# Delta-rule attention and a squared-Relu MLP on one core: the state's products with the queries moved behind T's second level, the key normalization moved to 0.45 to 0.80 of a period, and the weights' high words scaled in place

## The chip, the cores and the metric

The kernel runs on 1 core of one Trainium2 chip. The metric is the time of one execution on the device in microseconds (us). Before the change three runs took 672.78, 672.32 and 670.96 us (median 672.32).

## What is computed

Inputs are q, k and v of shape (4 batches, 8 heads, 768 tokens, 48), beta of shape (4, 8, 768), and two weight matrices. All arithmetic is to be that of float32; the weights are drawn in float64, so each of their elements is two 32-bit words.

```python
k_n = k / (np.linalg.norm(k, axis=-1, keepdims=True) + 1e-06)
for t in range(S):
    y[:, :, t] = einsum('bhd,bhde->bhe', q[:, :, t], state)
    v_old = einsum('bhde,bhd->bhe', state, k_n[:, :, t])
    state = state + beta_t * einsum('bhd,bhe->bhde', k_n[:, :, t], v[:, :, t] - v_old)
x = y.transpose(0, 2, 1, 3).reshape(B * S, H * D)      # 3072 x 384
h = maximum(x @ w_in, 0)                                # w_in 384 x 2048
out = (h * h) @ w_out                                   # w_out 2048 x 384
```

## The kernel before

**Chunks.** The 768 tokens are worked off in 12 units of 64 tokens. Within a unit the recurrence is written as matrix products: the keys' products with each other and with the queries (`static`, which also transposes keys and queries through TensorE and sends the blocks of the key products through DRAM), an inverse of a triangular matrix T per head, found by VectorE in 31 steps of two instructions on blocks of 32 (`invert`, lines 422 and 423), a second level that joins the blocks (`whole`), the products with the state carried over from the unit before (`on_state`), the solved values (`solved`), and the update of the state and the output (`onward`). The MLP (`moe`) then works on the 256 rows of the unit, with every operand split in a high and a low part, three products for one.

**Periods.** For unit `u` from 1 to 11 one period of the program weaves together: the MLP of unit u-1, the attention of unit u with the state, `static` and `invert` of unit u+1, and the loads and the key normalization of unit u+2. Each of these is a generator that gives up control after a piece of work, and each has a list of places between 0 and 1; `weave` sorts all pieces by place and writes them out in that order. The order on TensorE, VectorE, ScalarE and SyncE's DMA queue is this written order (`manual_schedule` names the four); GpSimd's is a scheduler's. The places are in 32nds for most parts: the MLP's pieces stand at 4/32 to 31/32 (its last ones in the next period, at 0/32 to 3/32 and 0.2), `static` at -1 and 4.9/32, the four pieces of the state part (`whole` in two, `solved`, `onward`) at 11.9/32, 15.9/32, 19.9/32 and 23.9/32, the inverse from 0.40 of one period to 0.12 of the next. In the period of unit 1 the rest of the weights is split too.

**Loads and normalization.** `loads(u)` first issues the keys of unit u+2 and the values of unit u+1, then the queries and beta, at two places between 0.22 and 0.42. Six places follow, N1, for the normalization: two of a square on ScalarE (line 270) with its sum on VectorE (271), the root on ScalarE (273), then VectorE's reciprocals and corrections (275 to 281) and the product that normalizes the keys (283). All loads of a period, the inverse's way through DRAM (`inv<-z`, `tt<-inv`, `t1t<-inv`), the blocks (`blocks<-ap`, `lt<-blocks`) and the output go through SyncE's queue, in the written order.

**The state part before the change.** At 11.9/32: 64 products for T's second level (line 461), ScalarE's copy of them, 64 products of the state with the queries into the bank `g`, 64 with the keys, and VectorE's subtraction of the latter from the values (501). At 15.9/32: the second 64 products of the level (471) and ScalarE's scaled copy of them into T's tile (475). At 19.9/32: T times the values (512) and its copy (514). At 23.9/32: the state's update (528, 531) and the output, added up in `g` (537, 541).

**The weights.** Each of 28 parts of the weights is loaded as pairs of words. `split_weights` makes a float32 high part and a low part of each: the absolute value of the high word on ScalarE (137), a maximum with 2^-15 on GpSimd (138), a shift and a mask on VectorE (145), the sign put back (148), the exponent alone (151), the low word scaled by it (152); then ScalarE and TensorE make the two parts (158, 165 to 167) and in the later parts VectorE takes a difference (172). The first 17 parts or so are split before the periods begin, the others in the period of unit 1.

Of the kernel before, what the change touches and what calls it, by code (L numbers as in the profile page):

```python
# [8 lines left out]
F32 = mybir.dt.float32  # L9
# [3 lines left out]
AF = mybir.ActivationFunctionType  # L13
ALU = mybir.AluOpType
AX = mybir.AxisListType

LEAST = 2.0 ** -15


@with_exitstack  # L20
def kernel(
# [22 lines left out]
    nc = tc.nc  # L44
    B, H, S, D = q.shape
    DM, DF = w_in.shape
    P = 128
    C = 64
    HB = 32
    NC = 2  # L50
    NP = H // 2
# [47 lines left out]
    state = const.tile([P, 2, NC, NP, D], F32, name="state")  # L99
# [11 lines left out]
    raws = []  # L111
# [14 lines left out]
    def room(x, n):  # L126
        pool, first, second = rooms[x % 2 if x < AHEAD - 1 else 0]
        return pool.tile([P, PC], I32, name=first)[:, :n], pool.tile([P, PC], I32, name=second)[:, :n]

    def split_weights():  # L130


        def least(x):

            w1 = raws[x][:, :, 1]
            a, rest = room(x, w1.shape[1])
            nc.scalar.activation(out=a.bitcast(F32), in_=w1.bitcast(F32), func=AF.Abs)  # L137
            nc.gpsimd.tensor_scalar(out=a.bitcast(F32), in0=a.bitcast(F32), scalar1=LEAST, scalar2=None, op0=ALU.max)  # L138
            return x, a, rest

        def words(x, a, rest):
            raw = raws[x]
            w1 = raw[:, :, 1]

            nc.vector.tensor_scalar(out=a, in0=a, scalar1=3, scalar2=0x3FFFFFF8,
                                    op0=ALU.logical_shift_left, op1=ALU.bitwise_and)

            nc.vector.scalar_tensor_tensor(out=a, in0=w1, scalar=-0x40000000, in1=a,  # L148
                                           op0=ALU.bitwise_and, op1=ALU.bitwise_or)

            nc.vector.tensor_scalar(out=w1, in0=a, scalar1=-0x800000, scalar2=None, op0=ALU.bitwise_and)
            nc.vector.scalar_tensor_tensor(out=rest.bitcast(F32R), in0=raw[:, :, 0].bitcast(U32), scalar=2.0 ** -52,
                                           in1=w1.bitcast(F32), op0=ALU.mult, op1=ALU.mult)
            return x, a, rest

        def high(x, a, rest):
            hl = wpool.tile([P, 2, raws[x].shape[1]], F32R, name=place[x])
            nc.scalar.copy(out=hl[:, 0], in_=a.bitcast(F32))
            return x, a, rest, hl

        def low(x, a, rest, hl, formed=False):
            ps = split_bank()[:, :hl.shape[2]]
            first = [(plus, hl[:, 1])] if formed else [(ident, a.bitcast(F32)), (minus, hl[:, 0])]
            for m, y in first:
                nc.tensor.matmul(ps, lhsT=m, rhs=y, start=(m is first[0][0]), stop=False)  # L165
            nc.tensor.matmul(ps, lhsT=plus, rhs=rest.bitcast(F32R), start=False, stop=True)
            nc.scalar.copy(out=hl[:, 1], in_=ps)
            halves[weight_parts[x][:2]] = hl[:, 0], hl[:, 1]

        def remainder(x, a, rest, hl):  # L170

            nc.vector.tensor_tensor(out=hl[:, 1], in0=a.bitcast(F32), in1=hl[:, 0].bitcast(F32), op=ALU.subtract)

        before, ready, x = None, [], 0
        while split_early:

            far = 3 if x < AHEAD - 3 else 1
            while len(ready) < far:
                ready.append(least(x + len(ready)))
            if x == 0:  # L180
                yield
            now = high(*words(*ready.pop(0)))
            if before:
                low(*before)
            before = now
            x += 1
            while len(ready) < (far if x < AHEAD - 3 else 1):
                ready.append(least(x + len(ready)))
            yield

        low(*before)
        before = None
        for x in range(x, NW):
            if before:
                remainder(*before)
            now = words(*ready.pop(0))
            yield
            if not ready and x + 1 < NW:
                ready.append(least(x + 1))
            yield  # L200
            if before:
                low(*before, formed=True)
            before = high(*now)
            yield
        remainder(*before)
        yield
        low(*before, formed=True)
        yield

    def split_bank():  # L210

        turn[1] += 1
        return (ps_o.tile([P, PC], F32, name=f"o{turn[1] % 2}") if split_early else ps_x.tile([P, PC], F32, name="x"))
# [72 lines left out]
    def x_tile(u=2):  # L286

        turn[0] += 1
        pool, name = (ps_h, "h") if u <= 1 and turn[0] % 4 >= 2 else (ps_x, "x")
        return pool.tile([P, PC], F32, name=name)  # L290
# [155 lines left out]
    def whole(d):  # L446

        u, ap = d["u"], d["ap"]
        tt = ttile[u % 2]
        upper = [slice(b * C, b * C + HB) for b in range(2)]  # L450
        lower = [slice(b * C + HB, (b + 1) * C) for b in range(2)]

        t1 = apool.tile([P, H, HB], F32, name="t1", bufs=1)
        nc.vector.transpose(out=t1, in_=d["t1t"])
        m = apool.tile([P, H, HB], F32, name="m", bufs=1)
        at = [upper, lower]
        ps = ps_h.tile([P, PC], F32, name="h")[:, :H * HB].rearrange("p (k t) -> p k t", k=H)
        for h in range(H2):
            c, e = h // H, h % H
            for b in range(2):  # L460
                nc.tensor.matmul(ps[at[h % 2][b], h // 2], lhsT=ap[lower[b], c, e, 0, :HB], rhs=tt[lower[b], c, e, HB:],
                                 start=True, stop=True)
        nc.scalar.copy(out=m, in_=ps)
        if u:
            on_state(d)
        yield
        ps = [x_tile(u)[:, :H * HB].rearrange("p (k t) -> p k t", k=H) for _ in range(2)]
        for h in range(H2):
            for b in range(2):
                rows = at[h % 2][b]  # L470
                nc.tensor.matmul(ps[h % 2][upper[b], h // 2], lhsT=t1[rows, h // 2], rhs=m[rows, h // 2], start=True, stop=True)  # L471
        right = tt.rearrange("p c (k j) t -> p j (c k) t", j=2)
        for j in range(2):
            for b in range(2):
                nc.scalar.mul(out=right[upper[b], j, :, HB:], in_=ps[j][upper[b]], mul=-1.0)  # L475
        yield

    def areas(two, n):

        return [x[:, :NC * n * D].rearrange("p (c n e) -> p c n e", c=NC, n=n) for x in two]  # L480

    def by_parity(x):

        return [x.rearrange("p c (n j) e -> p j c n e", j=2)[:, j] for j in range(2)]

    def on_state(d):

        kq, vt = d["kq"], d["vt"]
        d["g"] = g = ps_g.tile([P, 2, PC], F32, name="g")
        ks = areas([x_tile() for _ in range(2)], NP)  # L490
        for x, dst in ((1, areas([g[:, j] for j in range(2)], NP)), (0, ks)):
            for c in range(NC):
                for p in range(NP):
                    for j in range(2):
                        rows = slice(j * C, j * C + D)
                        for b in range(2):
                            to = slice((b ^ j) * C, ((b ^ j) + 1) * C)
                            nc.tensor.matmul(dst[j][to, c, p], lhsT=kq[rows, c, p, b, x], rhs=state[rows, b, c, p],  # L498
                                             start=(c == 0 and p == 0) if x else True, stop=not x, skip_group_check=True)
        for left, old in zip(by_parity(vt), ks):  # L500
            nc.vector.tensor_tensor(out=left, in0=left, in1=old, op=ALU.subtract)  # L501

    def solved(d):

# [146 lines left out]
    def state_part(d):  # L651
        yield from whole(d)
        solved(d)
        yield
        onward(d)
        yield
# [4 lines left out]
    STEPS = 32  # L661
    OVER = 4
    CHAIN = (11.9, 15.9, 19.9, 23.9)
    L1, N1 = (0.22, 0.42), (0.62, 0.92)
    I0, I1, NI = 0.40, 1.12, HB
    units = S // C
    ds_ = []
# [106 lines left out]
```

## Time and profile before

| | |
|---|---|
| runs | 672.78, 672.32, 670.96 us |
| profiled execution | 668.09 us, of which span 666.0 us |
| TensorE busy (matmuls) | 593.1 us, 89% of the span |
| VectorE busy | 434.7 us, 65% |
| ScalarE busy | 319.3 us, 48% |
| GpSimd busy | 73.7 us, 11% |
| TensorE's granted clock | 0.955 of full speed on average |
| moved by DMA | 49.92 MB in 173726 packets |

The profile names an instruction by the line of the kernel, its engine (PE is TensorE, PEld its loading of weights, DVE VectorE, ACT ScalarE, POOL GpSimd, SP SyncE, SPq the issue of a DMA on SyncE's queue), its operation, and the tiles it writes and reads. In a row of the timeline the first two numbers are the start and the time in us, and the brackets say how long the engine stood idle before it and what ended that. In a row of the groups stand the total busy time, the mean in ns, and the idle time before. In a row of the waits stand the total, the count and the longest. In a row of the stretches stand the stretch, its length, the busy time and count of PE, PEld, DVE, ACT and POOL, then the granted clock of TensorE, the DMA share and GB/s.

### The profile page before, as it was taken

The page shows a single profiled execution, that of the slowest core. Times are in us where ns is not written, and L with a number is a line of the kernel's source. Part 1 is how long each engine was busy: PE and PEld are TensorE (multiplying, and loading weights), DVE is VectorE, ACT ScalarE, POOL GpSimd, SP SyncE. Part 2 cuts the span into 40 slices and gives each one's busy share as a digit, 9 for nine tenths or more (in the row PEclk, how much of TensorE's full clock was granted, in tenths as well). Part 3 has the DMA queues.
Part 4 walks back from the last instruction along what each step waited for, and adds up shares of the span by engine and source line. Part 5 has one row for each costly group of instructions (what it writes and reads, how often), then busy time and mean ns, then how long its engine had stood idle before and what let it go on. Part 6 is the DMA issues. An engine that isn't in the chain of part 4 may idle for free.

```text
span 666.0 us, 23091 instructions
## 1 busy us (share of the span) xinstructions
PE 593.1 (89%) x9898; PEld 551.7 (83%) x9898; DVE 434.7 (65%) x1154; ACT 319.3 (48%) x620; POOL 73.7 (11%) x89
## 2 busy tenths in 40 slices
PE   0750788887999999999899999999999999999997
PEld 0530367887999899999899999999999998999996
DVE  4889887898568388397386595683883874841221
ACT  3740476564353453544355453544535554435442
POOL 6632333220100100101001001001001010000000
PEclk9965788788999999999899999999999999999999
DMA  7698622400450441532432523514514315030100
GB/s 157 158 234 298 198 52 46 77 2 1 72 112 10 95 89 19 103 69 34 100 55 39 102 49 56 112 22 78 104 23 104 68 28 111 2 65 2 25 1 25
DMA packets 173726, 49.92 MB, mean 75 GB/s; under 512 B 165424, under 2 KB 168504, under 8 KB 173624
## 3 DMA queue, kind: packets, MB, share of 16 engines
q1 hardware_dynamic: 171160, 47.85, 33.7%
q8 instruction: 78, 1.28, 0.8%
q10 hardware_dynamic: 2336, 0.59, 0.5%
q14 instruction: 24, 0.20, 0.1%
q0 software_dynamic: 128, 0.01, 0.0%
HBM read 37.32 MB, written 11.01 MB: 73 GB/s over the span
## 4 chain that ended last, share of the span: by engine, by line
PE 61%; DVE 19%; DMA 9%; SPq 4%; issue 4%; ACT 2%; DVEq 0%; ACTq 0%
PE h L588 24%; PE o L575 23%; DVE tmp L422 4%; DVE z L423 3%; DMA kpad<-in_k_dram 2%; DVE tt L423 2%; DVE h_h L420 2%; DVE h_l L567 2%; PE x L498 2%; PE g L498 1%; DMA blocks<-ap 1%; DMA inv<-z 1%; PE g L333 1%; DMA lt<-blocks 1%; PE x L333 1%
## 5 line engine op out<-in xcount | busy, mean ns | idle before, releaser
L575 PE MATMUL o<-w,h_h 128*128 128x384 f32 x768 | 200.0, 342 | 0.0
L588 PE MATMUL h<-x_h,w 128*128 128x256 f32 x1152 | 177.4, 290 | 0.0
L588 PEld LDWEIGHTS h<-x_h,w 128*128 128x128 f32 x1152 | 155.1, 193 | 3.6 <-issue 0.2
L595 ACT ACTIVATE r<-h 128x512 f32<-128x512 f32 x96 | 57.4, 598 | 194.5 <-PE h L588 193.9
L575 PEld LDWEIGHTS o<-w,h_h 128*128 128x128 f32 x768 | 136.3, 189 | 0.8
L567 DVE TENSOR_TENSOR h_l<-r,h_h 128x512 fp32r<-128x512 f32 x96 | 67.1, 699 | 99.1 <-PE o L575 61.2
L575 PE MATMUL o<-w,h_l 128*128 128x384 f32 x384 | 130.4, 340 | 0.0
L422 DVE SCALAR_TENSOR_TENSOR tmp<-lt,bt,z 128x126 f32<-128x126 f32 (+22 forms) x310 | 95.5, 308 | 50.7 <-DMA lt<-blocks 44.0
L588 PE MATMUL h<-x_l,w 128*128 128x256 f32 x576 | 100.9, 284 | 0.6 <-issue 0.6
L423 DVE TENSOR_TENSOR z<-z,tmp 128x126 f32<-128x126 f32 (+22 forms) x310 | 79.2, 255 | 10.7
L588 PEld LDWEIGHTS h<-x_l,w 128*128 128x128 f32 x576 | 83.2, 192 | 0.8 <-issue 0.8
L575 PEld LDWEIGHTS o<-w,h_l 128*128 128x128 f32 x384 | 72.5, 189 | 0.0
L596 ACT ACTIVATE r<-r 128x512 f32<-128x512 f32 x96 | 60.7, 633 | 3.0
L598 ACT CAST h_h<-r 128x512 fp32r<-128x512 f32 x96 | 59.6, 621 | 3.1
L406 POOL MEMSET z<- 128x512 f32 x10 | 5.3, 532 | 383.2 <-DMA inv<-z 383.2
L138 POOL TENSOR_SCALAR a<-a 128x384 f32<-128x384 f32 (+1 forms) x19 | 26.2, 1380 | 50.4 <-ACT a L137 46.5
L165 PE MATMUL o<-r,plus 128*128 128x512 f32 (+1 forms) x16 | 10.5, 745 | 18.6 <-DVE r L148 18.6
L501 DVE TENSOR_TENSOR vt<-vt,x 128x384 f32<-128x384 f32 x22 | 11.2, 549 | 15.2 <-PE x L498 15.2
L475 ACT ACTIVATE tt<-x 32x256 f32<-32x256 f32 x44 | 16.5, 374 | 9.6 <-PE x L471 9.0
L317 PE MATMUL x<-plus,kpad 64*128 64x64 f32 x104 | 7.8, 248 | 14.5 <-DMA kpad<-in_k_dram 12.4
L498 PE MATMUL x<-state,kq 48*64 48x48 f32 x704 | 14.1, 221 | 7.2 <-issue 7.2
L165 PEld LDWEIGHTS o<-r,plus 128*128 128x128 f32 x16 | 3.0, 234 | 20.2 <-ACT s L273 18.2
(134 smaller groups left out, 731.0 us busy)
## 6 DMA issues: line engine op xcount, KB each, us to landing
w<-in_moe_w_in_dram SPq DMA_DIRECT2D x12, 512.0 KB
w<-in_moe_w_out_dram SPq DMA_DIRECT2D x16, 384.0 KB
lt<-blocks SPq DMA_DIRECT2D x22, 256.0 KB
vt<-in_v_dram SPq DMA_DIRECT2D x48, 96.0 KB
out_dram<-a SPq DMA_DIRECT2D x46, 96.0 KB
kpad<-in_k_dram SPq DMA_DIRECT2D x88, 48.0 KB
qpad<-in_q_dram SPq DMA_DIRECT2D x88, 48.0 KB
blocks<-ap SPq DMA_DIRECT2D x48, 64.0 KB
```

The source lines that it names most:

```text
L138: nc.gpsimd.tensor_scalar(out=a.bitcast(F32), in0=a.bitcast(F32), scalar1=LEAST, scalar2=None, op0=ALU.max)
L165: nc.tensor.matmul(ps, lhsT=m, rhs=y, start=(m is first[0][0]), stop=False)
L422: nc.vector.scalar_tensor_tensor(out=tmp, scalar=bt[:, s:s + 1], op0=ALU.mult, op1=ALU.mult, **factors)
L423: nc.vector.tensor_tensor(out=z[:, :nj, s + 1:], in0=z[:, :nj, s + 1:], in1=tmp, op=ALU.subtract)
L475: nc.scalar.mul(out=right[upper[b], j, :, HB:], in_=ps[j][upper[b]], mul=-1.0)
L498: nc.tensor.matmul(dst[j][to, c, p], lhsT=kq[rows, c, p, b, x], rhs=state[rows, b, c, p], start=(c == 0 and p == 0) if x else True, stop=n ...
L567: nc.vector.tensor_tensor(out=h_l, in0=r, in1=h_h.bitcast(F32), op=ALU.subtract)
L575: nc.tensor.matmul(o[i], lhsT=a[:, e, i * P:(i + 1) * P], rhs=halves["wo", ft][w], start=(ft == 0 and n == 0), stop=(ft == FT - 1 and n == 2))
L588: nc.tensor.matmul(hp[:, e], lhsT=halves["wi", (kt, ft // EACH)][w][:, f], rhs=x[:, kt], start=(n == 0), stop=(n == 3 * KT - 1))
L595: nc.scalar.activation(out=r, in_=hp, func=AF.Relu)
L596: nc.scalar.activation(out=r, in_=r, func=AF.Square)
L598: nc.scalar.copy(out=h_h, in_=r)
```

## The change

Three things are changed. The products of the state with the queries go from the first piece of the state part to the second, behind the matmuls of line 471; `on_state` becomes a helper for either kind. The six places of the normalization go from 0.62 to 0.92 to 0.45 to 0.80 of the period. And the high word of each weight is no longer made absolute and bounded in a tile of its own: ScalarE multiplies it by 2^-112 in place, and VectorE shifts it from there; the sign is taken from the scaled word.

```diff
-LEAST = 2.0 ** -15
+DOWN = 2.0 ** -112
...
         def least(x):
-            w1 = raws[x][:, :, 1]
-            a, rest = room(x, w1.shape[1])
-            nc.scalar.activation(out=a.bitcast(F32), in_=w1.bitcast(F32), func=AF.Abs)
-            nc.gpsimd.tensor_scalar(out=a.bitcast(F32), in0=a.bitcast(F32), scalar1=LEAST, scalar2=None, op0=ALU.max)
-            return x, a, rest
-
-        def words(x, a, rest):
+            w1 = raws[x][:, :, 1].bitcast(F32)
+            nc.scalar.activation(out=w1, in_=w1, func=AF.Copy, scale=DOWN)
+            return x,
+
+        def words(x):
             raw = raws[x]
             w1 = raw[:, :, 1]
-            nc.vector.tensor_scalar(out=a, in0=a, scalar1=3, scalar2=0x3FFFFFF8,
-                                    op0=ALU.logical_shift_left, op1=ALU.bitwise_and)
-            nc.vector.scalar_tensor_tensor(out=a, in0=w1, scalar=-0x40000000, in1=a,
+            a, rest = room(x, w1.shape[1])
+            nc.vector.tensor_scalar(out=a, in0=w1, scalar1=3, scalar2=None, op0=ALU.logical_shift_left)
+            nc.vector.scalar_tensor_tensor(out=a, in0=w1, scalar=-0x80000000, in1=a,
                                            op0=ALU.bitwise_and, op1=ALU.bitwise_or)
...
         nc.scalar.copy(out=m, in_=ps)
         if u:
-            on_state(d)
+            keys_on_state(d)
         yield
...
                 nc.tensor.matmul(ps[h % 2][upper[b], h // 2], lhsT=t1[rows, h // 2], rhs=m[rows, h // 2], start=True, stop=True)
+        if u:
+            queries_on_state(d)
         right = tt.rearrange("p c (k j) t -> p j (c k) t", j=2)
...
-    def on_state(d):
-        kq, vt = d["kq"], d["vt"]
+    def on_state(d, x, dst):
+        for c in range(NC):
+            for p in range(NP):
+                for j in range(2):
+                    rows = slice(j * C, j * C + D)
+                    for b in range(2):
+                        to = slice((b ^ j) * C, ((b ^ j) + 1) * C)
+                        nc.tensor.matmul(dst[j][to, c, p], lhsT=d["kq"][rows, c, p, b, x], rhs=state[rows, b, c, p],
+                                         start=(c == 0 and p == 0) if x else True, stop=not x, skip_group_check=True)
+
+    def keys_on_state(d):
+        ks = areas([x_tile() for _ in range(2)], NP)
+        on_state(d, 0, ks)
+        for left, old in zip(by_parity(d["vt"]), ks):
+            nc.vector.tensor_tensor(out=left, in0=left, in1=old, op=ALU.subtract)
+
+    def queries_on_state(d):
         d["g"] = g = ps_g.tile([P, 2, PC], F32, name="g")
...
+        on_state(d, 1, areas([g[:, j] for j in range(2)], NP))
...
-    L1, N1 = (0.22, 0.42), (0.62, 0.92)
+    L1, N1 = (0.22, 0.42), (0.45, 0.80)
```

More of the change, by code (lines that the diff above doesn't have):

```diff
@@ L484, in by_parity @@
         return [x.rearrange("p c (n j) e -> p j c n e", j=2)[:, j] for j in range(2)]
-    def on_state(d):
-        kq, vt = d["kq"], d["vt"]
-        d["g"] = g = ps_g.tile([P, 2, PC], F32, name="g")
[L490 to L501, printed above, removed]
+    def on_state(d, x, dst):
[13 more added lines that the diff above has]
+    def queries_on_state(d):
+        d["g"] = g = ps_g.tile([P, 2, PC], F32, name="g")
+        on_state(d, 1, areas([g[:, j] for j in range(2)], NP))
     def solved(d):
```

## The prediction

> **What bounds the kernel now.** I read the page first, then who waited for whom between 168 us and 600 us (where the periods repeat), then one period queue by queue.
>
> ```profile
> span 666.0 us, 23091 instructions
> PE 593.1 (89%) x9898; PEld 551.7 (83%) x9898; DVE 434.7 (65%) x1154; ACT 319.3 (48%) x620; POOL 73.7 (11%) x89
> ...
> DVE tmp L422 <- DMA lt<-blocks: 44.0, 9, 6.2
> ACT rest L270 <- DMA kpad<-in_k_dram: 7.0, 5, 2.8
> PE x L498 <- issue: 5.2, 5, 2.0
> PE x L317 <- DVE kpad L283: 2.1, 3, 0.9
> ```
>
> The last two of these rows are nearly all of TensorE's idle time there: 7.3 us. So almost nothing can be won in the periods. But a second ring is as long as TensorE's. VectorE idles 44.0 us for the blocks `lt` that the inverse starts from. I follow that ring through one period, on SyncE's queue and then on VectorE:
>
> ```profile
> 261.73 1.29 SPq L429 DMA_DIRECT2D inv<-z  x2
> 275.90 1.14 SPq L359 DMA_DIRECT2D lt<-blocks  x2
> 277.14 2.98 SPq L616 DMA_DIRECT2D out_dram<-a  x4
> 280.16 6.72 SPq L232 DMA_DIRECT2D kpad<-in_k_dram  x8
> 308.10 1.29 SPq L429 DMA_DIRECT2D inv<-z  x2
> ```
> ```profile
> 280.79 0.25 DVE L422 SCALAR_TENSOR_TENSOR tmp<-lt,bt,z 128x31 f32<-128x31 f32 x1 [5.97 <-DMA lt<-blocks]
> 283.18 0.22 DVE L423 TENSOR_TENSOR z<-z,tmp 128x56 f32<-128x56 f32 x1
> 307.35 0.69 DVE L425 TENSOR_TENSOR z<-z,bt 128x512 f32<-128x512 f32 x1
> ...
> 280.79:308.10 27.31, 26.42 (x397) 25.22 (x399) 25.14 (x81) 12.99 (x25) 0.00 (x0) 1.00 0.27 50
> ```
>
> From the issue of `inv<-z` to the first use of `lt` are 19.06 us, and from there to the end of L425 27.25 us (VectorE, the third pair of numbers in the last row, busy 25.14 of it, the rest gaps between instructions). 19.06 + 27.25 is the 46.4 us between two `inv<-z`. The ring of SyncE's queue and VectorE is full, like TensorE.
>
> Also in that queue: the keys (`kpad`) are issued last, from 280.16 to 286.88, behind `lt` and the output. ScalarE reads them at once:
>
> ```profile
> 278.88 1.54 ACT L475 ACTIVATE tt<-x 32x256 f32<-32x256 f32 x4 [0.85 <-PE x L471]
> 281.21 0.60 ACT L595 ACTIVATE r<-h 128x512 f32<-128x512 f32 x1 [0.79 <-PE h L588]
> ...
> 288.02 0.53 ACT L270 ACTIVATE rest<-kpad 128x384 f32<-128x384 f32 x1 [2.76 <-DMA kpad<-in_k_dram]
> 288.45 0.58 ACT L595 ACTIVATE r<-h 128x512 f32<-128x512 f32 x1
> ...
> 290.25 0.52 ACT L270 ACTIVATE rest<-kpad 128x384 f32<-128x384 f32 x1
> ```
> ```profile
> 283.21 1.15 PE L512 MATMUL x<-vt,tt 64*64 64x48 f32 x64
> ...
> 286.16 0.52 PE L588 MATMUL h<-x_l,w 128*128 128x256 f32 x3
> ```
>
> L270 (the first square of the normalization) already waits 2.76 us for the keys. The Relu behind it (L595) could have run when its matmuls ended at 286.68, and ran at 288.45: what stands behind a waiting instruction waits too. Now it costs nothing, as TensorE is not that near.
>
> **The normalization moved.** Its six steps move from 0.645, 0.695, 0.745, 0.795, 0.845, 0.895 of a period to 0.479, 0.5375, 0.596, 0.654, 0.7125, 0.771 (six midpoints of 0.62 to 0.92, and of 0.45 to 0.80). The loads keep their places, and the SyncE queue above isn't touched, so the keys come when they come. The second part of the `whole` step stands at 15.9/32 = 0.497, so the first square is now ahead of L475, and its sum (L271) stands on VectorE after inverse steps at 0.411, 0.433, 0.456 and 0.478: four.
>
> When do the keys land, counted from `inv<-z`? L270's start, where it waited, tells it:
>
> ```profile
> 114.58 5.68 SPq L232 DMA_DIRECT2D kpad<-in_k_dram  x8
> ...
> 184.58 5.90 SPq L232 DMA_DIRECT2D kpad<-in_k_dram  x8
> ...
> 214.81 1.28 SPq L429 DMA_DIRECT2D inv<-z  x2
> ...
> 495.54 2.39 SPq L429 DMA_DIRECT2D inv<-z  x2
> 541.78 1.29 SPq L429 DMA_DIRECT2D inv<-z  x2
> ...
> 131.17 0.75 ACT L475 ACTIVATE tt<-x 32x256 f32<-32x256 f32 x2
> ...
> 240.71 0.53 ACT L270 ACTIVATE rest<-kpad 128x384 f32<-128x384 f32 x1 [0.61 <-DMA kpad<-in_k_dram]
> 520.52 0.53 ACT L270 ACTIVATE rest<-kpad 128x384 f32<-128x384 f32 x1 [0.37 <-DMA kpad<-in_k_dram]
> ```
>
> 25.9, 26.3 and 25.0 us: mean 25.7. The new place of L270 is reached before L475's present start, 17.2 us after `inv<-z` (278.88 - 261.73). ScalarE would stand some 8.5 us, with L475, the next Relu, and TensorE's L512, which needs L475's block, behind it. VectorE stands too: four inverse steps and one L567 are done 2.6 us after `lt` (280.79 to 283.40), then L271 waits for the square.
>
> The new ring, on VectorE: 25.7 to the keys; 0.55 for the square; the rest of the 27.25 without the 2.6 done early, 24.65. Then the second square: on ScalarE it stands behind L475 (1.54) and the next L595, L596, L598 (1.8, from 288.45 to 290.25), and takes 0.52, so it ends 4.4 after the keys land; VectorE gets to its sum after the first sum (0.56) and two inverse steps (1.2), at 2.3, and waits 2.1. Sum 25.7 + 0.55 + 24.65 + 2.1 = 53.0. Through TensorE the ring is shorter: 25.7, square and L475 2.2, and from L512 to the next `inv<-z` 24.9 (283.21 to 308.10): 52.8, less the 0.9 that L317 waits there. Both agree on about 53; I take VectorE's.
>
> From 214.81 to 541.78 are seven rings of 46.7 us on average. At 53.0 each, +6.3 x 7 = **+44**. The period before them (its keys' issue ends at 190.48; in the period above they were there 1.1 after it, 286.88 to 288.02; so 191.7) gives 191.7 + 0.55 + 24.65 + 2.1 = 219.0 in place of 214.81: **+4**. The last two periods load no keys, and the first (keys issued by 120.3, L475 at 131.17) has them in time. Bounds: with 25.0 to the keys and no second wait, 50.2 a ring, +25 and +2; with 26.3 and all waits, 53.6, +48 and +5.
>
> **The queries' products moved.** The same 64 matmuls, from between L461 and the keys' products to behind L471. Nothing is added. Now 192 small matmuls run in one go, and the 5.2 us of "issue" fall in their last third; after it they are two runs of 128. L528 and L537 are a run of 128 with next to none of that, so I expect these stalls to go. In the periods with the ring above that gains nothing, since TensorE waits at L512 anyway; in the tail, **-1**. (0 if runs of 128 stall as well; -7 if TensorE's ring stayed the longest, with the slow clock of rival B.) The bank `g` is asked for four steps later, so it makes no new wait; the keys' subtraction on VectorE comes a microsecond earlier.
>
> **The high words.** Abs on ScalarE becomes Copy with a scale, in place: same count (28), same size, I take the same time. GpSimd's maximum goes, and VectorE's shift reads every second word instead of a contiguous tile.
>
> ```profile
> L145 DVE TENSOR_SCALAR a<-a 128x384 int32<-128x384 int32 x11 | 4.9, 448 | 1.6 <-POOL a L138 1.6
> L145 DVE TENSOR_SCALAR r<-r 128x384 int32<-128x384 int32 x5 | 2.6, 521 | 1.4 <-POOL r L138 1.4
> L148 DVE SCALAR_TENSOR_TENSOR a<-w,a 128x512 int32<-128x512 int32 x8 | 5.5, 692 | 0.3
> L151 DVE TENSOR_SCALAR w<-r 128x512 int32<-128x512 int32 x4 | 1.7, 430 | 0.3
> ...
> 48.30 0.75 DVE L423 TENSOR_TENSOR tt<-tt,h_h 128x247 f32<-128x247 f32 x1
> 55.33 0.42 DVE L423 TENSOR_TENSOR tt<-tt,h_h 128x247 f32<-128x247 f32 x1
> 81.81 0.35 DVE L145 TENSOR_SCALAR a<-a 128x384 int32<-128x384 int32 x1
> 83.80 0.77 DVE L145 TENSOR_SCALAR r<-r 128x384 int32<-128x384 int32 x1
> ```
>
> VectorE's waits for GpSimd (first two rows): 3.0. While GpSimd works, some VectorE instructions take 0.3 to 0.4 longer (last four rows). The means of L145 here, 448 and 521 against 350 undisturbed, make 1.9 over 16, and its 12 wider ones may add 1; in the first inverse I count four such instructions for the maximum, 1.3. That is 7, a part of it while the first inverse goes through DRAM and VectorE is not what is waited for; I take **-5**. The shift with gaps in its input isn't shown; L151, which writes with gaps, takes 0.43, and L148, with two inputs, 0.69. I take L151's price, being one-input like it. At L148's (about +0.2 each on 28) the gain is gone. Bounds -9 and 0. The Trainium skill's "VectorE: DVE Perf Modes" ("What auto-detection actually checks") names a unit step for 16-bit operands alone, not for the mode that two ports give a single source; by it the shift stays at 0.43 and the -5 stands.
>
> **Sum.** The profiled execution took 668.1 (span 666.0 and 2.1 around it): 668.1 + 44 + 4 - 1 - 5 = 710. The median of the runs, 672.3, lies 4.2 above it, so **714** as a median.
>
> **Rivals.**
>
> A, the second wait isn't there or the ring has slack that I don't see: 50.2 a ring, 668.1 + 27 - 1 - 7 + 4.2 = 691. For it: only one of the periods quoted shows VectorE without a break.
>
> B, the clock. TensorE would stand 4 us and more in each period. The longest stall at L498 (2.0) ended at 321.5, and behind it stood:
>
> ```profile
> 322.00:324.00 2.00, 2.00 (x33) 1.95 (x26) 1.02 (x2) 0.00 (x0) 0.00 (x0) 0.63 0.27 53
> 324.00:326.00 2.00, 2.00 (x12) 2.00 (x11) 0.00 (x0) 0.00 (x0) 0.00 (x0) 0.52 0.69 212
> ```
>
> Granted 0.63 and 0.52 (the column before the last two) for 4 us: some 1.7 us of work lost ((0.37 + 0.48) x 2). Where TensorE's ring, 51.9 to 52.8, then passes VectorE's, it adds 0.6 to 1.6 to each of eight: up to 726. The Trainium skill's "TensorE: Matmul & The Clock Gate" ("HAM oscillation — how this bites in real kernels") has the clock halved after gaps of over 3.4 us; here 2.0 us did it.
>
> C, not slower: the keys are there in time. That needs them within 19.5 us of `inv<-z` (L475's start at 17.2, and the 2.8 from its end, 280.42, to L512 less 0.53 for the square), against the 25.0 to 26.3 seen. If it were so, the stalls at L498 and L317 (7.3), their slow clock (2), the first period's (2) and the 5 of the words would be won: 668.1 - 16 + 4.2 = 656. Nothing in the diff moves the queue.
>
> D, that it does nothing: the words' gain and a small stall cancel, 672.
>
> **Chances.** Forecast 0.58, A 0.13, B 0.16, C 0.10, D 0.03. A measurement of this kernel can tell 0.3% from no change. Faster 0.09, same 0.03, slower 0.88. The range leaves C and D out: 688 (A less 3) to 730 (B and the upper ends).
>
> **What would show it.** L270's first instance in each of the periods three to ten ahead of L475, with 6 us or more of waiting for the keys; `inv<-z` 53 us apart; L271 twice with a wait for ScalarE; TensorE idle at L512. "issue" at L498 gone; no L138; L145 near 0.43. I am wrong if the keys are issued earlier in the queue, or if `inv<-z` follows one another by 47 us despite the wait.

## The result and the profile after

The changed kernel takes 705.8 us (median of four runs, 700.7 to 709.3) against 671.6 before: the ratio is 1.0505, 95% interval 1.0435 to 1.0575. In a second comparison on one chip (below) it is 1.0557, 1.0507 to 1.0606. The forecast was 714, within 688 to 730, slower with a chance of 0.88.

The profiled execution took 700.7 (before 668.1). Some line numbers have shifted: the square is L268 (before L270), its sum L269 (L271), the inverse's step L420 (L422) and its last line L423 (L425), its way to DRAM L427 (L429), T times the values L518 (L512), the state's products with keys and queries L494 (L498), the normalizing product L281 (L283), the transposes L315 (L317), the shift L144 (L145). L475, ScalarE's copy into T's tile, has kept its number.

The page's first lines, and the waits from 168 to 640 us (total, count, longest). The last row is TensorE's only one there of a tenth of a microsecond or more:

```profile
span 699.0 us, 22990 instructions
PE 606.0 (87%) x9898; PEld 564.3 (81%) x9898; DVE 427.7 (61%) x1154; ACT 317.6 (45%) x620; POOL 35.0 (5%) x61
...
ACT rest L268 <- DMA kpad<-in_k_dram: 67.3, 8, 10.9
DVE n L269 <- ACT rest L268: 53.4, 16, 5.0
DVE tmp L420 <- DMA lt<-blocks: 39.7, 8, 7.3
...
PE x L518 <- ACT tt L475: 28.9, 16, 5.4
```

Three engines stand one after the other: ScalarE for the keys (7.0 us before, 67.3 now; 8.4 a period on average, where 8.5 was predicted), VectorE for ScalarE's squares (16 waits: two in each of eight periods), TensorE for the block that ScalarE makes behind the square. The issue stalls at the state's products are gone. One period on SyncE's queue, then on ScalarE, VectorE and TensorE (start, duration, and in brackets the idle time before):

```profile
213.93 1.28 SPq L427 DMA_DIRECT2D inv<-z  x2
228.27 1.87 SPq L357 DMA_DIRECT2D lt<-blocks  x2
230.24 2.50 SPq L622 DMA_DIRECT2D out_dram<-a  x4
232.78 6.19 SPq L230 DMA_DIRECT2D kpad<-in_k_dram  x8
...
267.62 1.28 SPq L427 DMA_DIRECT2D inv<-z  x2
...
317.92 1.29 SPq L427 DMA_DIRECT2D inv<-z  x2
...
575.08 1.29 SPq L427 DMA_DIRECT2D inv<-z  x2
```
```profile
240.11 0.52 ACT L268 ACTIVATE rest<-kpad 128x384 f32<-128x384 f32 x1 [10.87 <-DMA kpad<-in_k_dram]
240.54 1.52 ACT L475 ACTIVATE tt<-x 32x256 f32<-32x256 f32 x4
243.91 0.52 ACT L268 ACTIVATE rest<-kpad 128x384 f32<-128x384 f32 x1
290.71 0.52 ACT L268 ACTIVATE rest<-kpad 128x384 f32<-128x384 f32 x1 [6.85 <-DMA kpad<-in_k_dram]
...
240.67 0.55 DVE L269 TENSOR_REDUCE n<-rest 128x8 f32<-128x384 f32 x1 [4.71 <-ACT rest L268]
244.46 0.55 DVE L269 TENSOR_REDUCE n<-rest 128x8 f32<-128x384 f32 x1 [2.14 <-ACT rest L268]
266.87 0.69 DVE L423 TENSOR_TENSOR z<-z,bt 128x512 f32<-128x512 f32 x1
...
241.34 0.45 PE L518 MATMUL x<-vt,tt 64*64 64x48 f32 x4 [5.42 <-ACT tt L475]
242.12 1.94 PE L518 MATMUL x<-vt,tt 64*64 64x48 f32 x60 [0.33 <-ACT tt L475]
```

The first fence shows the order, keys last behind the inverse, the blocks and the output, and the second shows that the square waits for them with L475 behind it. The rings from 213.93 to 575.08 are seven in 361.2 us, 51.6 each, where before they took 46.7. Compared by the starts of `inv<-z`: the first is at 163.09 (before 169.06), 6.0 earlier; the next period is 5.1 longer (50.84 against 45.75; before it could be read from 169.06 to 214.81); the seven rings are 34.2 longer; the rest to the end is 0.3 shorter. That is the 33 us between the two spans.

### The profile page after: what moved, and what is told of

Read it like the earlier page. It is cut to its first block, busy times and chain, and to the rows that moved or that the text cites. A ratio compares the mean times of both kernels' runs of the same rounds, so it can differ in the third digit from the quotient of the medians.

```text
span 699.0 us, 22990 instructions
## 1 busy us (share of the span) xinstructions
PE 606.0 (87%) x9898; PEld 564.3 (81%) x9898; DVE 427.7 (61%) x1154; ACT 317.6 (45%) x620; POOL 35.0 (5%) x61
## 4 chain that ended last, share of the span: by engine, by line
PE 76%; DMA 9%; SPq 5%; DVE 4%; ACT 4%; issue 2%; ACTq 0%; DVEq 0%
PE h L594 30%; PE o L581 27%; DMA kpad<-in_k_dram 4%; SPq L230 3%; PE x L518 2%; DMA w<-in_moe_w_out_dram 2%; ACT tt L475 2%; PE x L331 2%; PE x L494 2%; PE x L534 2%; PE o L163 1%; PE g L494 1%; PE g L331 1%; PE g L543 1%; DMA inv<-tt 1%
## 5 line engine op out<-in xcount | busy, mean ns | idle before, releaser
L594 PE MATMUL h<-x_h,w 128*128 128x256 f32 x1152 | 182.3, 296 | 0.0
L594 PEld LDWEIGHTS h<-x_h,w 128*128 128x128 f32 x1152 | 159.8, 199 | 3.8 <-issue 0.2
L420 DVE SCALAR_TENSOR_TENSOR tmp<-lt,bt,z 128x126 f32<-128x126 f32 (+22 forms) x310 | 95.5, 308 | 49.8 <-DMA lt<-blocks 39.7
L594 PE MATMUL h<-x_l,w 128*128 128x256 f32 x576 | 103.1, 289 | 0.0
L594 PEld LDWEIGHTS h<-x_l,w 128*128 128x128 f32 x576 | 85.7, 198 | 0.0
L269 DVE TENSOR_REDUCE n<-rest 128x8 f32<-128x384 f32 x20 | 10.9, 552 | 60.4 <-ACT rest L268 60.4
L518 PE MATMUL x<-vt,tt 64*64 64x48 f32 x704 | 21.8, 267 | 28.9 <-ACT tt L475 28.9
L518 PEld LDWEIGHTS x<-vt,tt 64*64 64x64 f32 x704 | 18.9, 180 | 33.1 <-ACT tt L475 32.6
L268 ACT ACTIVATE rest<-kpad 128x384 f32<-128x384 f32 x20 | 10.2, 519 | 74.7 <-DMA kpad<-in_k_dram 74.7
L547 ACT COPY y<-g 128x384 f32<-128x384 f32 x24 | 10.3, 483 | 24.1 <-PE g L543 24.1
L341 DVE TENSOR_TENSOR ap<-x,mask 128x512 f32<-128x512 f32 x20 | 12.9, 686 | 11.5 <-PE x L331 11.5
```

Of the source, the lines that this page charges most:

```text
L420: nc.vector.scalar_tensor_tensor(out=tmp, scalar=bt[:, s:s + 1], op0=ALU.mult, op1=ALU.mult, **factors)
L518: nc.tensor.matmul(tv[j][to, c, p], lhsT=tt[rows, c, h], rhs=vt[rows, c, h], start=True, stop=True)
L594: nc.tensor.matmul(hp[:, e], lhsT=halves["wi", (kt, ft // EACH)][w][:, f], rhs=x[:, kt], start=(n == 0), stop=(n == 3 * KT - 1))
```

## The experiments

Each is compared with the kernel before on the same chip, whose median was 668.2, 669.6 and 668.2 us in the three groups.

### Each part alone

```diff
 e1_norm_only: the kernel before with
-    L1, N1 = (0.22, 0.42), (0.62, 0.92)
+    L1, N1 = (0.22, 0.42), (0.45, 0.80)
 e2_all_but_norm: the changed kernel with
-    L1, N1 = (0.22, 0.42), (0.45, 0.80)
+    L1, N1 = (0.22, 0.42), (0.62, 0.92)
 e3_words_only: the kernel before with the changed least() and words()
 e4_queries_only: the kernel before with the changed on_state() and its two callers
```

> The kernel before with one edit: the normalization at 0.45 to 0.80. Theory (the squares stand ahead of L475 and wait for keys that SyncE's queue brings late, which lengthens the ring of that queue and VectorE): the whole loss and none of the gains. In the changed kernel the seven rings from 213.93 to 575.08 took 34.2 more than before and the period ahead of them 5.1 more, so 671.6 + 39 = 711, at least 703. Rival (the loss comes from the queries' products or the words, the move of the normalization is harmless): within 4 us of 671.6.

> The changed kernel with the normalization back at 0.62 to 0.92. Theory: no loss, the gain of the words (the first inverse of the periods left 6.0 earlier in the changed kernel: 163.09 against 169.06) and some of the stalls at L498: 659 to 666. Rival (the queries' products or the words cost): 672 or more. TensorE should have no wait for L475's block at its products with the values, and no issue stall of 1 us or more in the state's products.

> The kernel before with the words' edit alone. Theory: 6.0 us less than before up to the first inverse of the periods, then the same periods: 665.6, between 662 and 669. Rival (the early gain is lost again in the periods, whose ring of SyncE and VectorE isn't touched, or came from the moved normalization in the first period): within 2 us of 671.6.

> The kernel before with the queries' products behind the second level alone. Theory (the periods are bound by the ring of SyncE's queue and VectorE, 19 + 27.1 = 46.1 at the least, as much as by TensorE): the stalls at L498 go (5.2 in the periods, 2.0 in the first), of which some 0.6 a period can be won, 46.7 to 46.1: 5 us at the most, so 666 to 671. Rival (TensorE alone bounds the periods): stalls and the slow clock behind them are won in full, 662 to 664. Rival (a run of 128 stalls as well): 671.6.

| kernel | median, us | ratio to before | 95% interval |
|---|---|---|---|
| normalization alone | 711.4 | 1.0689 | 1.0618 to 1.0759 |
| all but the normalization | 658.9 | 0.9887 | 0.9856 to 0.9918 |
| words alone | 664.8 | 0.9962 | 0.9931 to 0.9992 |
| queries alone | 663.1 | 0.9940 | 0.9903 to 0.9977 |

TensorE's waits over the periods, with the normalization alone (two rows), the words alone (two), the queries alone (one), and all but the normalization (two):

```profile
PE x L512 <- ACT tt L475: 24.8, 16, 5.4
PE x L498 <- issue: 4.2, 4, 1.7
```
```profile
PE x L496 <- issue: 5.0, 5, 1.7
PE x L315 <- DVE kpad L281: 2.9, 4, 1.3
```
```profile
PE x L317 <- DVE kpad L283: 4.9, 7, 1.4
```
```profile
PE x L315 <- DVE kpad L281: 4.9, 4, 2.5
PE g L494 <- issue: 0.4, 1, 0.4
```

The whole loss is the normalization's: alone it costs 6.9%, and without it the other two win 1.1%. The queries' move ends the stalls at the state's products, as the third and fourth fence show (0.4 are left of 4 to 5). It wins 4.0 us (1.5 to 6.5 by the interval). That is within the 5 at the most that was expected, though the interval goes past it; it stays short of the 7.2 of stalls that the rival, TensorE alone, would have won in full. The words win 2.5 us, 0.5 to 4.6, which is less than the 6 expected; the 6.0 us by which the first `inv<-z` left earlier in the changed kernel (163.09 against 169.06) are therefore not the words' alone.

### Keys early, squares back

```diff
 e5_keys_early (changed kernel): the keys' load at the start of the period, the values with the queries
-            parts += [(getting, steps(2, *L1) + steps(6, *N1)), ...
+            parts += [(getting, [0.001, 0.37] + steps(6, *N1)), ...
...
         if u + 2 < units:
             ds_.append(load(u + 2))
+        yield
         if u + 1 < units:
             load_v(ds_[u + 1])
-        yield
         if u + 2 < units:
             load_q(ds_[u + 2])
 e6_squares_back (changed kernel): two squares at their places of before, the four steps behind them at 0.72 to 0.78
+            parts += [(getting, steps(2, *L1) + [0.645, 0.695, 0.72, 0.74, 0.76, 0.78]), ...
```

> The changed kernel with the keys' load alone moved to the start of the period (0.001), ahead of the inverse's way through DRAM in SyncE's queue; the values go with the queries. The normalization stays at 0.45 to 0.80. Theory: no wait for keys at L268, no idle TensorE at the products with T, rings of 46 to 47 us; as the changed kernel without the moved normalization (0.9887 of before, so 659 where before is 668), or 2 to 4 less, since the late L281 no longer holds up the transposes (4.9 us in that kernel): 654 to 660. Rival (the squares and sums cost by their place, ahead of the level's copy and between the inverse's first steps, whether they wait or not): rings of 50 and more, 680 or more.

> The changed kernel with the two squares back at 0.645 and 0.695, and the other four steps at 0.72, 0.74, 0.76, 0.78, so that the normalization still ends by 0.80. Theory (the two squares alone do the harm): 654 to 661. Rival (the later steps at 0.596 to 0.771 do part of it): above 665.

Keys early: 658.7 us, ratio 0.9838 (0.9797 to 0.9878). Squares back: 657.3, ratio 0.9803 (0.9762 to 0.9843). In the first the normalization stands exactly where it stands in the changed kernel. All of TensorE's waits in its periods, and two rows of the second kernel (ScalarE's wait for keys, and TensorE's longest in total):

```profile
PE g L494 <- issue: 0.3, 1, 0.3
PE h L459 <- DMA tt<-inv: 0.2, 1, 0.2
```
```profile
ACT rest L268 <- DMA kpad<-in_k_dram: 15.1, 6, 3.5
PE h L459 <- DMA tt<-inv: 0.7, 3, 0.4
```

So the place costs nothing by itself, only the wait that it lets ScalarE and VectorE run into. And the later four steps are better early: at 0.62 to 0.92 the product L281 held the transposes up by 4.9 us, and that kernel is at 0.9887, with an interval clear of the 0.9803 here, though measured on another chip. Squares late and the rest early is the fastest kernel measured here, 2.0% faster than before (1.6 to 2.4) and 6.7% faster than the changed one (0.9803/1.0505), but not clear of the keys early, whose interval overlaps with its own; ScalarE still waits 15.1 us for keys in it, with nothing pressing behind.

### What sets the length of a ring

```diff
 all on the changed kernel
 e7_squares_together
+            parts += [(getting, steps(2, *L1) + [0.479, 0.485, 0.596, 0.654, 0.7125, 0.771]), ...
 e8_values_first: load_v(ds_[u + 1]) ahead of ds_.append(load(u + 2)) in loads()
 e9_second_square_late
+            parts += [(getting, steps(2, *L1) + [0.479, 0.60, 0.63, 0.66, 0.7125, 0.771]), ...
 e10_square_behind
+            parts += [(getting, steps(2, *L1) + [0.50, 0.5375, 0.596, 0.654, 0.7125, 0.771]), ...
```

> The changed kernel with the second square moved up from 0.5375 to 0.485, next to the first, so that it no longer stands behind L475 and the next Relu. Theory as predicted (VectorE's ring, in which the second sum waits 2.14 us in each of eight periods): the wait goes, 17 us less than the changed kernel (0.975 to 0.98 of it). Rival (TensorE's ring is nearly as long: L475 now waits for both squares, and behind the standstill the clock is halved): 0 to 8 us less.

> The changed kernel with the values' load ahead of the keys' in SyncE's queue: the keys come 2.6 us later (four issues, 2.63 in the trace). Theory (the keys' landing is on the ring): 2.6 x 8 = 21 us more than the changed kernel, 15 to 25 with what is hidden by landing together. Rival (something else, as the clock or VectorE alone, sets the period): less than 5 more.

> The changed kernel with the second square at 0.60 in place of 0.5375 (the root at 0.63, the next step at 0.66), so that VectorE comes to its sum after it is done, and nothing new stands ahead of L475. Theory (VectorE's ring is the longer one, TensorE's some 1 us shorter: from the first square to the next inverse 27.2 against 2.0 + 24.2): the wait of 2.14 in each of eight periods goes, TensorE's ring then decides: 6 to 10 us less than the changed kernel. Rival (TensorE's ring is just as long, so the second wait cost nothing): within 2 us of the changed kernel.

> The changed kernel with the first square at 0.50, just behind L475 in place of just ahead of it. TensorE's products with T then don't wait for keys; VectorE's sum still does. Theory (both rings run through the keys' wait; with TensorE's free, VectorE's is left, with five inverse steps ahead of the sum in place of four and a shorter wait at the second: 50.2 against 51.6): 8 to 14 us less than the changed kernel, still over 685. Rival (what counts is L475 held back): as with the squares at their old places, 655 to 665. Rival (VectorE alone counts): no TensorE waits and the same rings of 51.6, within 3 us of the changed kernel.

> The changed kernel itself, for the comparison with the two kernels beside it on one chip: 1.04 to 1.06 of before.

| kernel | median, us | ratio to before | 95% interval |
|---|---|---|---|
| changed, as it is (same chip as the last two) | 705.9 | 1.0557 | 1.0507 to 1.0606 |
| squares together | 707.8 | 1.0570 | 1.0532 to 1.0608 |
| values ahead of keys | 730.8 | 1.0912 | 1.0868 to 1.0957 |
| second square late | 700.4 | 1.0467 | 1.0402 to 1.0532 |
| first square behind L475 | 698.7 | 1.0456 | 1.0390 to 1.0522 |

Values ahead of keys: 2.6 us later in the queue is 24 to 27 us more (1.0912 less 1.0557 or 1.0505, of 670), 3.0 to 3.4 a period, at and above the upper end of the 15 to 25 expected. In its trace the first square stands 27.4 us behind `inv<-z` on average, where it stands 24.2 and 24.7 in the two traces of the changed kernel; its rings are 54.8 (219.24 to 602.85) where theirs are 51.6 and 52.0. Both grow by the same 3.2, or 2.7 and 2.8: the keys' landing is on the ring with its full length. TensorE's and ScalarE's waits rise with it (28.9 and 67.3 in the changed kernel):

```profile
ACT rest L268 <- DMA kpad<-in_k_dram: 92.6, 8, 13.5
PE x L518 <- ACT tt L475: 53.4, 16, 8.2
```

The second square is a different matter. With the squares together the second wait is nearly gone (below: 3.61 for the first sum, 0.45 for the second), and nothing is won, where the theory expected 17 us and its rival up to 8:

```profile
347.31 0.52 ACT L268 ACTIVATE rest<-kpad 128x384 f32<-128x384 f32 x1 [9.04 <-DMA kpad<-in_k_dram]
348.31 0.52 ACT L268 ACTIVATE rest<-kpad 128x384 f32<-128x384 f32 x1 [0.48 <-DMA kpad<-in_k_dram]
348.74 1.53 ACT L475 ACTIVATE tt<-x 32x256 f32<-32x256 f32 x4
...
347.87 0.55 DVE L269 TENSOR_REDUCE n<-rest 128x8 f32<-128x384 f32 x1 [3.61 <-ACT rest L268]
348.87 0.55 DVE L269 TENSOR_REDUCE n<-rest 128x8 f32<-128x384 f32 x1 [0.45 <-ACT rest L268]
```

From the first square (347.31) the next `inv<-z` came 27.2 later (374.52); over the seven rings it is 27.0 to 28.3, mean 27.7, and not less than the 27.4 of the changed kernel. L475 starts 1.4 us after the first square in place of 0.4, so TensorE's ring is that much longer. That this is what eats the gain is argued, not shown; what the trace shows is that VectorE waits elsewhere instead, 36.3 us in all for the MLP's high parts `h_h` from ScalarE (30.1 in the second trace of the changed kernel) and 15.4 for TensorE's `x` at L341 (10.1). With the second square late L475 stays where it was, and VectorE has one wait a period (eight, not sixteen):

```profile
DVE n L269 <- ACT rest L268: 34.7, 8, 5.1
PE x L518 <- ACT tt L475: 27.8, 16, 4.9
```

That measured 0.9% less than the changed kernel beside it, 6 us, with intervals that overlap; its rings are 51.2 us on average (215.04 to 573.69), where the changed kernel's on that chip are 52.0 (215.91 to 580.14), 0.8 less where the wait was 2.1. Of the 0.8, 0.3 are keys that landed earlier behind `inv<-z` (24.4 against 24.7); from the first square to the next `inv<-z` it is 26.8 against 27.3, so 0.5 of the 2.1 was won. In the two rings in which TensorE's 60 products of L518 ran at full clock (1.14 us) this stretch took 26.1, in the five at half clock (1.95) 26.3 to 27.7. In this one trace, then, what is behind the wait is about a microsecond shorter at full clock, and the slow clock takes most of that back.

With the first square behind L475 the products with T don't wait any more, and yet it wins only 1.0%. TensorE's only long wait has gone one piece further, to the state's update, which needs the solved values that ScalarE copies (L520) behind the same squares:

```profile
298.39 0.52 ACT L268 ACTIVATE rest<-kpad 128x384 f32<-128x384 f32 x1
...
299.65 0.84 ACT L520 COPY vt<-x 128x384 f32<-128x384 f32 x2
```
```profile
PE x L534 <- ACT vt L520: 21.5, 7, 3.6
```

None of the three expectations had that. The middle one, that L475 alone counts, falls clearly; of the others neither is confirmed. The time is 7 us less, with 8 to 14 expected and intervals that overlap with the changed kernel's, and the rings are 51.3 (220.52 to 579.84, in the slowest of its four runs), nearer the 51.6 of the rival than the 50.2 of the theory. Yet the theory's step was right: from the first square to the next `inv<-z` it is 25.8 in every ring (from 296.03 to 321.82, say), about 1.5 less than in the changed kernel, although TensorE waits. What hid it is the other term: the keys landed 25.6 behind `inv<-z` on average, 0.8 to 1.3 later than in the two traces of the changed kernel. Why they landed later stays open.

## Why the prediction was right, point by point

**The cause and its sign** were right. The keys' landing is not moved by the change, ScalarE reaches the square before it, and what stands behind it waits: run for run, by the normalization alone (+6.9%), by the keys early (gone), by the values first (keys 2.7 to 3.2 us later made rings 2.8 to 3.2 longer). The keys early also make rival C's condition true: priced at 656 of 672, it measured 0.9838, which is 661.

**The ring.** Predicted 25.7 from `inv<-z` to the keys and 27.3 from there to the next; 53.0. The second term was exact. From the seven first squares (240.11, 290.71, and so on to 547.78) to the next `inv<-z` it is 27.2 to 27.6, mean 27.4, and VectorE's second wait 2.14 for the 2.1 worked out. The mis-sized term is the first: 26.2 (213.93 to 240.11), 23.1 (267.62 to 290.71), and by turns so on, mean 24.2. In the rows above, the issue of `lt` comes 14.3 after `inv<-z`; in the next ring it comes 11.6 after it:

```profile
271.24 2.21 SPq L436 DMA_DIRECT2D tt<-inv  x4
...
279.23 1.58 SPq L357 DMA_DIRECT2D lt<-blocks  x2
```

The load back from DRAM could be issued 3.6 us after `inv<-z` at 267.62 here, and 5.2 in the period ahead (213.93 to 219.08); before the change it took 5.0 in the period that the prediction read, and 4.5 to 5.2 in all seven of its rings. Here it took 3.6 in four of seven, in the second trace of the changed kernel in two of seven, where the first term is 24.7 and the ring 52.0. So the alternation is not fixed by the program, and why it is sometimes faster stays open. In the profiled execution the short first term makes 1.4 of the error per ring, 10 of the 44 in all: seven rings cost 34.2. The period ahead of them cost 5.1, where 4 were predicted.

**The second wait** was there with its size, but the sum took it as if it were all on the path. Rival A dropped it and would have had 50.2 a ring. The two squares' runs show neither: with TensorE's ring set at 51.9 to 52.8 beside 53.0, there was little to win, and taking the wait away won 0.5 of 2.1. (Rival A's 691 takes 7 off for the words where the sum takes 5; with 5 it would be 693.)

**Rival B, the clock.** TensorE did come back at half speed. In the changed kernel, stretch by stretch (the granted clock is the third number from the end), behind a standstill of 4.4 us:

```profile
342.00:344.00 2.00, 0.07 (x2) 0.07 (x4) 0.73 (x2) 1.25 (x4) 0.00 (x0) 0.98 0.51 94
344.00:346.00 2.00, 1.67 (x52) 1.51 (x56) 0.81 (x4) 1.90 (x5) 0.00 (x0) 0.50 0.80 145
346.00:348.00 2.00, 2.00 (x30) 1.91 (x23) 0.91 (x3) 1.38 (x4) 0.00 (x0) 0.50 0.47 84
348.00:350.00 2.00, 2.00 (x12) 2.00 (x11) 1.86 (x7) 0.60 (x2) 0.00 (x0) 0.50 0.29 50
350.00:352.00 2.00, 2.00 (x12) 2.00 (x12) 1.83 (x8) 1.13 (x2) 0.00 (x0) 0.82 0.39 72
352.00:354.00 2.00, 2.00 (x82) 1.76 (x84) 1.79 (x5) 0.72 (x2) 0.00 (x0) 1.00 0.02 3
```

Half speed for over 6 us is 3 us of work, more than the 1.7 assumed. But the ring hardly felt it: 27.4 from that first square (342.71) to the next `inv<-z`, and 27.2 in the period (496.02 to 523.22) in which the clock stayed up. VectorE, with its 27.3, is what the end of the ring waits for, so the slow clock fell on time that TensorE would have waited. With the second square late, where VectorE's wait is gone, it did count (26.1 at full clock, up to 27.7 at half).

**The queries** were set at 0 in the rings and 1 in the tail, because TensorE would wait there anyway. The tail is 0.3 shorter. Their worth without the loss (0.6%, queries alone) lay inside the bounds given, 0 to 7.

**The words** were set at 5 within 0 to 9; alone they measure 2.5 (0.5 to 4.6). The price taken for the shift was right: reading every second word it takes 413 and 355 ns, where 430 was taken, so the bound of 0.69 is far.

```profile
L144 DVE TENSOR_SCALAR a<-w 128x384 int32<-128x384 int32 x11 | 3.9, 355 | 0.8 <-ACT w L136 0.8
L144 DVE TENSOR_SCALAR a<-w 128x512 int32<-128x512 int32 x8 | 3.3, 413 | 0.0
```

The Trainium skill's "VectorE: DVE Perf Modes" ("What auto-detection actually checks"), which names no unit step for this case, agrees with that. The over-estimate is in how much of VectorE's saved time lay on the path. With the words alone VectorE's busy time fell by 6.9 us (434.7 to 427.8), about the 7 that the prediction counted, but its wait for the first inverse's way back from DRAM (`t1t<-inv`) rose from 0.5 to 4.1. The first `inv<-z` of the periods (169.06 before) came at 163.09 and 164.91 in the two traces of the changed kernel, at 167.71 with the words alone, 167.88 with the queries alone, 170.90 with the normalization alone and 166.44 with all but it. With one trace for each part, that hints that the three edits act together there; this was not taken apart.

**The sum** was 710 in the profiled execution's terms, and 700.7 was measured: the seven rings make 10 less, the start up to the first inverse 1 less, the period behind it 1 and the tail 0.7 more.

## What to carry to other kernels

An instruction that waits for a transfer is also a place in its engine's queue: before moving it forward, look for when the transfer lands (the queue's last issue, and where the reader waits now) and what will stand behind it. Here ScalarE was half idle, and two squares of 0.5 us at the wrong place cost 7%. Where two rings are within a microsecond or so of each other, taking a wait off one of them wins little, and moving the waiting instruction a step further only hands the wait to the next consumer; move the load, or leave the reader late and bring only its followers forward.

## What wasn't expected of the hardware

TensorE's clock fell to half behind standstills of very different length. The 60 products of L518 take 1.14 us at full clock and 1.95 at half; in the changed kernel's eight periods they took 1.95 behind gaps of 5.4, 5.3, 4.4 and 3.6, but also behind 1.7 and 1.8, and 1.14 behind 2.0 and 1.5. Behind the gap of 2.0 the clock fell all the same, only after the products: it was 0.58 from 190 to 192 us. Behind 1.5 it stayed up:

```profile
187.95 0.32 PE L518 MATMUL x<-vt,tt 64*64 64x48 f32 x4 [1.99 <-ACT tt L475]
188.73 1.14 PE L518 MATMUL x<-vt,tt 64*64 64x48 f32 x60 [0.47 <-ACT tt L475]
...
190.00:192.00 2.00, 2.00 (x12) 2.00 (x12) 0.89 (x3) 1.38 (x4) 0.00 (x0) 0.58 0.43 77
...
291.94 0.32 PE L518 MATMUL x<-vt,tt 64*64 64x48 f32 x4 [1.70 <-ACT tt L475]
292.72 1.95 PE L518 MATMUL x<-vt,tt 64*64 64x48 f32 x60 [0.47 <-ACT tt L475]
```

The 3.4 us that the Trainium skill's "TensorE: Matmul & The Clock Gate" ("HAM oscillation — how this bites in real kernels") names as the gap that halves it is thus no lower bound here: the gaps of 3.6 and more always did it, those of 1.7 to 2.0 did too, and the one of 1.5 did not. And two runs of 128 small products stalled TensorE for 0.4 us in all (all but the normalization), runs of 192 for 5.2 over the same periods before; why the longer run stalls wasn't tested.
